# Routing by 32x32 block transposes, two score buffers for the first pairs, and one of five sums left to an accumulating DMA

## The chip, the cores and the metric

The kernel runs on one core of a Trainium2 chip. The metric is the device time of one execution in microseconds (us); lower is better. Engines: TensorE (PE, matmuls; its weight loads are shown apart as PEld), VectorE (DVE), ScalarE (ACT), GpSimd (POOL) and SyncE (SP), which issues most DMAs.

## The reference

Two stages. The first is attention in which a query sees only the keys of its own cluster; the second is a gated long convolution over the sequence. B, H, S, D = 4, 8, 768, 64; 16 centroids per head; model width 512.

```
q_assign = argmax(normalized q . normalized centroids)     # likewise k_assign
scores   = where(q_assign == k_assign, q k^T / 8, -1e9)
attn     = exp(scores - max) / sum
x        = (attn v), heads side by side                     # 4 x 768 x 512
x1, x2, x3 = split(x @ w_proj)
y        = x1 * irfft(rfft(x2) * rfft(filter)) * x3         # over the 768 steps
out      = y @ w_out                                        # float32
```

## The kernel before, in words

**Pairs and steps.** The 32 (batch, head) items are taken as 16 pairs of heads (p = 0 to 15, four pairs per batch). A pair has six steps of 128 keys (`attend`, sk = 0 to 5). A step computes the scores of 128 keys against 768 queries for both heads into three PSUM banks (L687, the matmuls through the helper `halves` at L324, which splits each into two of 64 columns), one exponential of 128x1536 on ACT into a buffer pb (L689; three such buffers), the products with v accumulated over the six steps in two other banks (PV, L699), and from the second step on a sum acc += pb on DVE (L709), five per pair, which gives the softmax denominators.

**Routing** (`routing`, L593 to L668). Per pair: q and k are loaded into raw (L384), transposed on PE (L606) and copied into qkT; POOL casts them into aug (L313). Similarities to the centroids are matmuls (L623) laid out as four groups of 32 partitions (query/key by half of the sequence). Then ACT or DVE copies them to sim (L626), PE transposes that in three blocks of 128 (L631), DVE takes the maximum and makes a one-hot with ties broken by a reversed index (L636 to L642), PE transposes the one-hot in six blocks (L650), and DVE or ACT scales it by mk into ohT (L655, L657): the query side becomes +-262144, the key side 0 or 1. Four DMAs (L664) put ohT's rows into aug beside q and k, so that the score matmul adds a large negative number where clusters differ; the scores wait for them.

**Finish** (`finish`, L715). Matmuls with ones sum acc over the keys (L728), and for pairs 0 to 14 the denominators go out and back through DRAM in five DMAs on SP (L733 to L740) with the reciprocal between (L736). The last pair does this with DVE's block transpose (L752, L762) instead. The normalized output becomes sums and differences uT (L769) and a bf16 copy xT.

**Second stage** (`hyena`, L775), once per batch after its four pairs: projections u, a real transform as matmuls (F) with DVE products tm and their sum, gates (G) into x13, an inverse transform in two parities pe and po (I, 16 matmuls per block of 128 columns, L853), which ACT copies (od) and DVE adds and subtracts (L860), the gate product (L863), and the output matmuls with w_out. `angles`, `inverse_tables` and `filter_tables` build the transform tables at the start.

**The order.** Nothing here is in the order in which it is written. Each piece is an `op` with engines that may take it, an estimated duration, dependences and a due time; `Plan.run` (L175) schedules all of them by a list, simulating engines, buffers and PSUM banks with those estimates, and issues the instructions in that order. Dues are worked back from each step's (`step`, L375). The constants at L26 to L30 set paces, the weight of waiting (WAIT) and a bonus for keeping the PE tile shape (SAME). Each engine then runs its own queue in order, with semaphores for the dependences. `BankPool.choices` (L92) says which of eight PSUM banks a value may use: scores only 0 to 2, PV 3 and 4, the rest 5 to 7 and whatever is left over before the first scores and after the last.

Of the kernel before, what the change touches and what calls it, by code (L numbers as in the profile page):

```python
# [13 lines left out]
F32 = mybir.dt.float32  # L14
# [15 lines left out]
SAME, WAIT, ANGLES = 1.08, 82.17, 0.99  # L30
# [44 lines left out]
class Banks:  # L75

    def __init__(self, scores, outs, rest):
        self.views = [scores[:, 512 * n:512 * n + 512] for n in range(3)]  # L80
        self.views += [outs[:, 512 * n:512 * n + 512] for n in range(2)] + rest
        self.whole = {"S": scores, "O": outs}
        self.free, self.owner = [0.0] * 8, [None] * 8
        self.scores_left = self.scores_begun = 0
        self.outs_left = 0


class BankPool:
# [3 lines left out]
    def choices(self):  # L92
        b, k = self.b, self.kind
        if k == "S":
            return [(0, 1, 2)]
# [7 lines left out]
        if not b.scores_left:  # L103
            ok += [0, 1, 2]
# [12 lines left out]
    def take(self, v, c):  # L117
        for n in c:
            self.b.owner[n] = v
        t = self.b.views[c[0]] if len(c) == 1 else self.b.whole["O" if c[0] == 3 else "S"]  # L120
# [12 lines left out]
class Op:  # L133
    __slots__ = ("alts", "fn", "deps", "succ", "need", "due", "vals", "takes", "mode", "lag", "size",
                 "end", "n", "shared", "ready", "kind", "after", "left", "table")


class Plan:
# [5 lines left out]
    def __init__(self):  # L144
        self.ops = []

    def op(self, engine, dur, fn, r=(), w=(), due=1e9, takes=(), mode=None, size=0, shared=False,
# [4 lines left out]
        o.left, o.table = left or mode, table  # L152
# [112 lines left out]
def kernel(  # L265
# [55 lines left out]
    def halves(out, lhsT, rhs, **k):  # L321

        for c in range(2):
# [7 lines left out]
    mk = const("mk", [64, 2])  # L331
# [5 lines left out]
    hm = const("hm", [128, 3, 4, DM], BF16)  # L337
    zeroed = Val(Pool("zeroed", [None]))
# [9 lines left out]
    ohTp = pool("ohT", 2, [64, S], BF16)  # L348
# [21 lines left out]
                  [psum.tile([128, 512], F32, name=f"bank{i}") for i in range(3)])  # L370
    psS, psO, psF, psD, psE = (BankPool(banks, x) for x in ("S", "O", "F", "D", "E"))
    banks.scores_left, banks.outs_left = NP * NT, NP
# [16 lines left out]
    def load_pair(p):  # L389
        b, h = p // 4, 2 * (p % 4)  # L390
        for j, src in enumerate((q, k)):
            x = raws[p, j] = Val(raw)
            for hp in range(2):
                load(lambda x=x, hp=hp: x.t[:, :, hp], src[b, h + hp].rearrange("(p t) d -> p t d", t=NT),
                     196608, step(6 * p - LOAD) + j if p else -1000.0, (x, hp),
                     after=step(6 * p - LOAD) - 8.0 if p > 1 else 0.0, behind=masks0)
        x = vraws[p] = Val(vraw)
# [4 lines left out]
    def constants():  # L402
        op("POOL", 0.5, lambda e: make_identity(nc, identp.t), w=[identp], kind="const")
# [3 lines left out]
        for g, (a, c) in enumerate(((BIG, -BIG), (1.0, 0.0))):  # L407
            def f(e, g=g, a=a, c=c):
                nc.gpsimd.memset(mk.t[32 * g:32 * g + 32, 0:1], a)
                nc.gpsimd.memset(mk.t[32 * g:32 * g + 32, 1:2], c)  # L410
# [4 lines left out]

    def zeros():
        def f(e):
# [9 lines left out]
    def centroid():  # L427
        small = {n: const(n, [128, w]) for n, w in
# [25 lines left out]
    def angles():  # L454


        N = 2 * 192
        na, ra = Val(k6), Val(k6)
# [19 lines left out]
        for m in range(3):  # L478
            n = lambda m=m: na.t[:, N * (m + 1):N * (m + 2)]
            r = lambda m=m: ra.t[:, N * m:N * (m + 1)]  # L480
            due = ANGLES + 1.5 * m
            op("DVE", 0.36, lambda e, m=m, n=n: V.tensor_scalar(n(), kc(), st.t[:, m:m + 1], None, op0=Alu.mult),
               r=[(na, "k"), st], w=[(na, m)], due=due)
            op("DVE", 0.36, lambda e, n=n, r=r: V.tensor_scalar(r(), n(), 1.0 / S, MAGIC, op0=Alu.mult, op1=Alu.add),
               r=[(na, m)], w=[(ra, m)], due=due)
            op("DVE", 0.36, lambda e, r=r: V.tensor_scalar(
                r(), r(), MAGIC, -float(S), op0=Alu.subtract, op1=Alu.mult), r=[(ra, m)], w=[(ra, m)], due=due)
            op("DVE", 0.56, lambda e, n=n, r=r: V.tensor_tensor(n(), n(), r(), op=Alu.add),
               r=[(ra, m)], w=[(na, m)], due=due, shared=True)
            done.append(op("DVE", 0.56, lambda e, n=n, r=r: V.scalar_tensor_tensor(  # L490
                r(), n(), -1.0, n(), op0=Alu.mult, op1=Alu.max), r=[(na, m)], w=[(ra, m)], due=due, shared=True))
        two = lambda x: x.rearrange("p (a b) -> p a b", a=2)
# [15 lines left out]
    def inverse_tables(due):  # L508
        for j in range(6):
            ps = Val(psF)  # L510

            def f(e, j=j, ps=ps):
# [11 lines left out]
               r=[ps], w=[inv], due=due + j + 1)  # L524

# [10 lines left out]
    def filter_tables(due):  # L536
        lo, hi, ud = Val(k6), Val(k6), Val(k6)
# [7 lines left out]
        op("DVE", 1.76, lambda e: nc.vector.tensor_tensor(fu(), lo.t, hi.t, op=Alu.add),  # L545
           r=[lo, hi], w=[(ud, 0)], due=due, shared=True)
        op("DVE", 1.76, lambda e: nc.vector.tensor_tensor(fd(), lo.t, hi.t, op=Alu.subtract),
# [10 lines left out]
        V = nc.vector  # L558
        for i in range(3):
            for cs in range(2):  # L560
                ps = Val(psF)
# [4 lines left out]
                op("DVE", 0.68, lambda e, i=i, cs=cs, ps=ps, w=w: V.tensor_scalar(  # L566
                    hm.t[:, i, 2 * cs], ps.t, w(), None, op0=Alu.mult), r=[ps, wt], w=[(hm, (i, 2 * cs))],
                   due=due + 2 * i + cs)
                if i == 0 and cs == 0:
                    op("DVE", 0.68, lambda e, ps=ps: V.tensor_scalar(  # L570
                        d1.t[:, 0], ps.t, wt.t[:, 1:2], None, op0=Alu.mult), r=[ps, wt], w=[d1], due=due)
# [4 lines left out]
                elif cs == 0:  # L576
                    op("DVE", 0.68, lambda e, i=i, ps=ps: V.tensor_scalar(
                        hm.t[:, i, 3], ps.t, 2.0 / S, None, op0=Alu.mult), r=[ps], w=[(hm, (i, 3))],
# [355 lines left out]
```

## Time and profile before

| what | us |
| --- | --- |
| median of 3 runs | 423.12 (422.86 to 423.76) |
| the profiled execution's own time | 422.92 |
| its span in the trace | 421.1 |
| PE busy / DVE busy / ACT busy / POOL busy | 393.9 / 354.4 / 256.5 / 120.9 |

The mean granted PE clock of the span is 0.984. A row of a group reads: line, engine, operation, output and inputs with shapes, count, then busy time in us and the mean of one in ns, then the idle time of the engine ahead of it and what ended that. A row in order of time reads: start in us, duration, engine, line, operation and count, and in brackets the idle time before it. The queue of SP shows as SPq.

### The profile page before, as it was taken

What the parts mean: (1) busy time and instruction counts of PE and PEld (TensorE: products, weight loads), DVE (VectorE), ACT (ScalarE), POOL (GpSimd) and SP (SyncE); (2) the same over time, 40 slices, a digit from 0 to 9 for tenths busy, and PEclk for the clock granted to TensorE, in tenths of its full rate; (3) what the DMA queues carried; (4) which work ended last, traced back from release to release, by engine and by line L of the source; (5) the groups of instructions that cost most, each with busy time, mean ns of one, the idle gap of its engine ahead of it and who ended that gap; (6) DMA issues with size and microseconds to landing.
All of it is one profiled execution on the core that took longest, in us unless ns stands there. A gap on an engine that the chain in (4) does not pass through costs nothing. (4 is left out here: it accounts for less than half of the span.)

```text
span 421.1 us, 8711 instructions
## 1 busy us (share of the span) xinstructions
PE 393.9 (94%) x3485; PEld 213.6 (51%) x3485; DVE 354.4 (84%) x414; ACT 256.5 (61%) x317; POOL 120.9 (29%) x114
## 2 busy tenths in 40 slices
PE   4489998999999999999999999999999999998794
PEld 2245444445445565655454545545655467555442
DVE  5959977898989898989879799999899788947673
ACT  2477655888577767555775766666676654344242
POOL 5722333155253140532405051407113002101000
PEclk9869999999999999999999999999999999999998
DMA  8199956544363314020365711110311002200123
GB/s 183 20 226 216 222 128 148 129 99 93 87 158 86 84 45 115 10 77 3 76 161 161 164 40 48 48 40 4 84 41 40 3 10 81 101 2 2 75 76 149
DMA packets 68943, 37.17 MB, mean 88 GB/s; under 512 B 56940, under 2 KB 62632, under 8 KB 68904
## 3 DMA queue, kind: packets, MB, share of 16 engines
q1 hardware_dynamic: 67640, 34.45, 31.9%
q0 software_dynamic: 1056, 2.10, 2.7%
q8 instruction: 27, 0.44, 0.4%
q10 hardware_dynamic: 208, 0.08, 0.1%
q14 instruction: 12, 0.10, 0.1%
HBM read 30.66 MB, written 6.48 MB: 88 GB/s over the span
## 5 line engine op out<-in xcount | busy, mean ns | idle before, releaser
L689 ACT ACTIVATE pb<-scores 128x1536 f32<-128x1536 f32 x96 | 139.4, 1452 | 52.2 <-PE scores L324 50.9
L699 PE MATMUL outs<-pb,vraw 128*64 128x512 f32 (+1 forms) x768 | 143.2, 492 | 0.2 <-ACT osb L719 0.2
L313 POOL CAST aug<-qkT 64x768 bf16<-64x768 f32 x64 | 85.1, 1329 | 160.6 <-PE scores L324 80.3
L709 DVE TENSOR_TENSOR acc<-acc,pb 128x1536 f32<-128x1536 f32 x64 | 118.1, 1845 | 9.5 <-ACT pb L689 9.1
L699 PEld LDWEIGHTS outs<-pb,vraw 128*64 128x64 f32 x768 | 54.4, 137 | 66.2 <-issue 59.7
L324 PE MATMUL scores<-aug,aug 128*64 128x512 bf16 (+3 forms) x768 | 81.8, 332 | 5.1 <-DMA aug<-ohT 2.8
L324 PEld LDWEIGHTS <-aug 80*64 80x64 bf16 (+1 forms) x768 | 42.1, 111 | 35.0 <-issue 15.5
L324 PEld LDWEIGHTS <-wpj 128*64 128x64 bf16 x512 | 32.3, 110 | 16.6 <-issue 5.6
L324 PE MATMUL bank<-xT,wpj 128*64 128x384 bf16 x384 | 38.5, 326 | 0.0
L709 DVE TENSOR_TENSOR acc<-pb,pb 128x1536 f32<-128x1536 f32 x16 | 31.8, 1987 | 4.7 <-ACT pb L689 4.7
L606 PE MATMUL bank<-ident,raw 128*128 128x128 f32 x183 | 30.5, 294 | 5.5 <-DMA raw<-in_q_dram 5.4
L324 PEld LDWEIGHTS <-k 128*64 128x64 bf16 (+1 forms) x448 | 21.7, 108 | 22.3 <-issue 11.4
L863 POOL TENSOR_TENSOR k<-yy,x 128x768 bf16<-128x768 f32 x7 | 16.1, 2302 | 58.6 <-DVE yy L860 54.1
L606 PEld LDWEIGHTS bank<-ident,raw 128*128 128x128 f32 x183 | 20.6, 147 | 20.1 <-issue 11.5
L311 ACT COPY qkT<-bank 128x384 f32<-128x384 f32 x47 | 21.8, 482 | 10.3 <-PE bank L606 10.2
L313 POOL CAST xT<-rb 128x768 bf16<-128x768 f32 x8 | 10.6, 1325 | 45.3 <-PE bank L324 20.1
L769 DVE TENSOR_TENSOR uT<-rb 128x384 bf16<-128x384 f32 x32 | 21.4, 680 | 0.1
L324 PE MATMUL bank<-wpj,uT 128*64 128x512 bf16 x160 | 20.6, 380 | 0.0
L804 DVE TENSOR_TENSOR tm<-bank,hm 128x1024 f32<-128x1024 f32 x16 | 19.4, 1219 | 0.8 <-PE bank L533 0.7
L719 ACT COPY osb<-outs 128x769 f32<-128x769 f32 x16 | 12.8, 801 | 8.9 <-PE outs L699 8.9
L764 DVE SCALAR_TENSOR_TENSOR rb<-osb,rb 128x768 f32<-128x768 f32 x16 | 17.8, 1114 | 0.0
L324 PEld LDWEIGHTS <-uT 128*64 128x64 bf16 x192 | 12.6, 109 | 8.6 <-issue 1.9
(161 smaller groups left out, 440.6 us busy)
## 6 DMA issues: line engine op xcount, KB each, us to landing
raw<-in_q_dram SPq DMA_DIRECT2D x32, 192.0 KB
raw<-in_k_dram SPq DMA_DIRECT2D x32, 192.0 KB
vraw<-in_v_dram SPq DMA_DIRECT2D x16, 384.0 KB
rb<-dr SPq DMA_DIRECT2D x30, 192.0 KB
out_dram<-os SPq DMA_DIRECT2D x21, 256.0 KB
k<-in_moe_filter_fft_dram SPq DMA_DIRECT2D x4, 384.0 KB
wpj<-in_moe_w_proj_dram POOLq DMA_DIRECT2D x1, 1536.0 KB, 14.3
aug<-ohT SPq DMA_DIRECT2D x62, 24.0 KB
```

The source lines that it names most:

```text
L311: nc.scalar.copy(o, i)
L313: eng[e].tensor_copy(o, i)
L324: nc.tensor.matmul(out[64 * c:64 * c + 64], lhsT[:, 64 * c:64 * c + 64], rhs, **k)
L606: nc.tensor.transpose(ps.t[:, ts(t, 128)], rv[:, 3 * ch + t], identp.t)
L689: op("ACT", 1.48, lambda e: nc.scalar.activation(pb.t[:, :, :S], sps.t.rearrange("p (a b) -> p a b", a=2), Act.Exp, scale=0.125), r=[sps], ...
L699: nc.tensor.matmul(o.t[64 * hp:64 * hp + 64, lo:hi], vv.t[:, hp, ts(sk, D)], pb.t[:, hp, lo:hi], start=(sk == 0), stop=(sk == NT - 1))
L709: nc.vector.tensor_tensor(acc.t, a, pb.t[:, :, :S], op=Alu.add)
L719: op("ACT", 0.82, lambda e: nc.scalar.copy(osb.t, o.t[:, :S + 1]), r=[o], w=[osb], due=step(i) + 5.0)
L764: op("DVE", 0.98, lambda e: V.scalar_tensor_tensor(rb.t, osb.t[:, :S], osb.t[:, S:S + 1], rb.t, op0=Alu.add, op1=Alu.mult), r=[osb, rb], w ...
L769: op("DVE", 0.55, lambda e, e_=e_, alu=alu: V.tensor_tensor(uT.t[:, e_], x3()[:, :, :64], x3()[:, :, 64:], op=alu), r=[rb], w=[(uT, e_)], ...
L804: op("DVE", 1.2, lambda e, i=i, cs=cs, ps=ps, tm=tms[cs]: V.tensor_tensor(tm.t, ps.t.unsqueeze(1).to_broadcast([128, 2, DM]), hm.t[:, i, c ...
L863: op(("DVE", "POOL"), (0.95, 1.8), lambda e, dt=dt, yt=yt, x13=x13: eng[e].tensor_tensor(y2v()[:, dt], yt().rearrange("p t c -> p (t c)"), ...
```

## The change

- **Routing.** The similarities go from PSUM to sim by DVE's transpose of 32x32 blocks; because they are laid out in groups of 32 partitions, this is all that the maximum needs. The one-hot goes back the same way. PE's two transposes and ACT's copy are gone. ohT becomes 128x384 (was 64x768), mk is scaled in place, and eight DMAs of half the length place the mask.
- **First scores.** In the first 24 steps scores may also use banks 5 to 7, and other values may use 0 to 2.
- **Sums.** In pairs 0 to 14 the fifth sum (sk = 5) is a DMA issued by POOL that adds pb into acc.
- **Inverse.** For batch 3, each parity is six matmuls straight into PSUM, with negated tables (`minus`, made on POOL), and DVE multiplies by x13 from PSUM; no od, yy or separate product.
- **Start.** 8 and 6 pairs of warm-up matmuls on the identity (`warm`); POOL may do parts of `angles` and of the filter's sum and difference, ACT parts of `filter_tables`.
- **Order.** Every op has a tag, and a table NUDGE adds a number to its due time; SAME is 2.358 (was 1.08), WAIT 145.939 (was 82.17).

```
+DIRECT = (3,)
+ADDED = (5,)
+TWICE = 24
+SAME, WAIT, ANGLES = 2.358, 145.939, 0.99
+NUDGE = {
+    "const": -13.63, "cent": -14.24, "l0.0": -135.15, "l0.1": -111.3, "v0": 25.44, "l1.0": -76.86,
...
+        o.due += NUDGE.get(o.tag, 0.0)
...
         if k == "S":
-            return [(0, 1, 2)]
+            return [(0, 1, 2)] + ([(5, 6, 7)] if b.scores_begun < b.twice else [])
...
-        if not b.scores_left:
+        if not b.scores_left or 0 < b.scores_begun < b.twice:
             ok += [0, 1, 2]
...
+    def warm(at, n, due):
+        for _ in range(n):
+            ps = Val(psE)
+            def f(e, ps=ps):
+                halves(ps.t, identb.t, identb.t.unsqueeze(1).to_broadcast([128, 4, 128]), start=True, stop=True)
+            op("PE", 0.43, f, r=[identb], w=[ps], due=due, after=at, mode="C64", kind="warm")
...
-        op(("ACT", "DVE"), (0.486, 0.55), lambda e: copy(e, sim.t, ps.t[:, :384]), r=[ps], w=[sim], due=due)
-                nc.tensor.transpose(sT.t[:, ts(t, 128)], sim.t[:, ts(t, 128)], identp.t)
+        op("DVE", 0.56, lambda e: nc.vector.transpose(sim.t, ps.t[:, :384]), r=[ps], w=[sim], due=due, kind="T1")
...
-                nc.tensor.transpose(tp[:64, t * 128:(t + 1) * 128], ov[:, t % 3, t // 3], identb.t)
+        op("DVE", 0.55, lambda e: V.transpose(ohT.t, oh.t.rearrange("p n c -> p (n c)")), r=[oh], w=[ohT], due=due,
+           kind="T2")
...
-        op(("DVE", "ACT"), (0.68, 0.815), f, r=[oT, mk], w=[ohT], due=due)
+        op(("DVE", "ACT"), (0.22, 0.48), f, r=[mk, ohT], w=[ohT], due=due)
...
-                    eng[e].dma_start(aug.t[hp][j][64 - 16 * hp:80 - 16 * hp], ohT.t[r0:r0 + 16])
+                for ch in range(2):
+                        r0 = 64 * ch + 32 * j + 16 * hp
+                        eng[e].dma_start(aug.t[hp][j][64 - 16 * hp:80 - 16 * hp, ts(ch, 384)], ohT.t[r0:r0 + 16])
...
-            op("DVE", 1.75, f, r=[pb] + ([last] if sk == 1 else [acc]), w=[acc], due=step(i) + 5.0,
-               shared=True, kind="acc")
+            if sk in ADDED and p < NP - 1:
+                op("POOL", 1.1, lambda e: nc.gpsimd.dma_start(acc.t, pb.t[:, :, :S], accum_op=Alu.add),
+                   r=[pb, acc], w=[acc], due=step(i) + 4.0, lag=7.0, kind="accD")
...
+            if b in DIRECT:
+                for e_ in range(2):
+                        for n in range(6):
+                            w = minus.t[:, n - 2] if e_ and n > 1 else inv.t[:, n]
+                            halves(ps.t[:, :384], yv()[:, n // 2, n % 2, ts(dt, 128)], w, start=(n == 0), stop=(n == 5))
...
+    warm(0.0, 8, FIRST - 300.0)
     routing(0)
+    warm(14.0, 6, T0 - 4.0)
```

More of the change, by code (lines that the diff above doesn't have):

```diff
@@ L79, in __init__ @@
     def __init__(self, scores, outs, rest):
[L80 to L82 removed]
+        self.views = [x[:, 512 * n:512 * n + 512] for x, m in ((scores, 3), (outs, 2), (rest, 3)) for n in range(m)]
+        self.whole = {0: scores, 3: outs, 5: rest}
         self.free, self.owner = [0.0] * 8, [None] * 8
[L84 removed]
+        self.scores_left = self.scores_begun = self.twice = 0
         self.outs_left = 0
@@ L134 @@
     __slots__ = ("alts", "fn", "deps", "succ", "need", "due", "vals", "takes", "mode", "lag", "size",
-                 "end", "n", "shared", "ready", "kind", "after", "left", "table")
+                 "end", "n", "shared", "ready", "kind", "after", "left", "table", "tag")
 class Plan:
@@ L369 @@
     banks = Banks(psum.tile([128, 1536], F32, name="scores"), psum.tile([128, 1024], F32, name="outs"),
-                  [psum.tile([128, 512], F32, name=f"bank{i}") for i in range(3)])
+                  psum.tile([128, 1536], F32, name="rest"))
     psS, psO, psF, psD, psE = (BankPool(banks, x) for x in ("S", "O", "F", "D", "E"))
-    banks.scores_left, banks.outs_left = NP * NT, NP
+    banks.scores_left, banks.outs_left, banks.twice = NP * NT, NP, TWICE
     def step(i):
@@ L720, in finish @@
         V = nc.vector
+        P.tag = f"den{p}"
         if p < NP - 1:
```

193 lines of the change are left out of this document (117 added, 76 removed), and 68 rows, old and new, of the table NUDGE.

## The prediction

> **What bounds the kernel now.** The first view is the page: busy time by engine, then the slices of the span.
>
> ```profile
> PE 393.9 (94%) x3485; PEld 213.6 (51%) x3485; DVE 354.4 (84%) x414; ACT 256.5 (61%) x317; POOL 120.9 (29%) x114
> ...
> PE   4489998999999999999999999999999999998794
> ...
> PEclk9869999999999999999999999999999999999998
> ```
>
> TensorE (PE) is busy for 393.9 of 421.1 us, and its row of tenths is full except at both ends. VectorE (DVE) is the runner-up with 84%. The averages hide stages, so the second view is the table of busy time by stretch; its columns are stretch, length, then PE, weight loads, DVE, ACT and POOL with counts, the granted PE clock and the DMA share.
>
> ```profile
> 80.00:100.00 20.00, 20.00 (x157) 9.22 (x153) 18.30 (x18) 15.86 (x17) 9.89 (x6) 1.00 0.38 85
> ...
> 360.00:380.00 20.00, 18.85 (x204) 11.16 (x200) 13.28 (x22) 8.43 (x16) 0.02 (x1) 1.00 0.14 52
> 380.00:400.00 20.00, 15.31 (x162) 10.00 (x157) 14.72 (x15) 6.77 (x15) 1.81 (x1) 1.00 0.11 40
> ```
>
> In the middle PE has no gap at all, at full clock, while DVE is at 18.3 of 20. In 360 to 400 PE is idle for 1.15 + 4.69 = 5.84 us: there the last batch waits for chains on DVE. So an instruction taken from PE in the middle is worth its whole time, one taken from DVE is worth nothing until something on PE or ACT waits for it, and the ends are about latency.
>
> **What leaves PE.** The routing loses its two transposes on PE: three of the similarities (L631) and six of the one-hots (L650) in each of 16 pairs. From the groups by line and shape:
>
> ```profile
> L709 DVE TENSOR_TENSOR acc<-acc,pb 128x1536 f32<-128x1536 f32 x64 | 118.1, 1845 | 9.5 <-ACT pb L689 9.1
> ...
> L631 PE MATMUL bank<-ident,sim 128*128 128x128 f32 x45 | 8.2, 291 | 0.0
> L650 PE MATMUL bank<-identb,oh 128*64 128x128 bf16 x90 | 7.9, 226 | 1.3 <-DVE oh L642 1.3
> ...
> L655 ACT ACTIVATE ohT<-bank,mk 64x768 bf16<-64x768 bf16 x7 | 6.9, 981 | 0.3 <-PE bank L650 0.3
> ...
> L311 ACT COPY sim<-bank 128x384 f32<-128x384 f32 x13 | 6.2, 478 | 7.9 <-PE bank L623 7.9
> ...
> L657 DVE TENSOR_SCALAR ohT<-bank,mk 64x768 bf16<-64x768 bf16 x8 | 5.3, 667 | 2.9 <-PE bank L650 2.8
> ...
> L752 DVE STREAM_TRANSPOSE acc<-scores 128x768 f32<-128x768 f32 x1 | 1.0, 983 | 1.4 <-PE scores L324 1.4
> ```
>
> Busy times of matmuls overlap, so I take distances between starts, in order of time:
>
> ```profile
> 150.15 1.59 PE L699 MATMUL outs<-pb,vraw 128*64 128x512 f32 x8
> 151.67 0.55 PE L631 MATMUL bank<-ident,sim 128*128 128x128 f32 x3
> 152.15 0.84 PE L324 MATMUL scores<-aug,aug 80*64 80x512 bf16 x8
> ...
> 166.63 1.46 PE L699 MATMUL outs<-pb,vraw 128*64 128x512 f32 x8
> 167.92 0.82 PE L324 MATMUL bank<-xT,wpj 128*64 128x384 bf16 x8
> ...
> 169.22 0.39 PE L650 MATMUL bank<-identb,oh 128*64 128x128 bf16 x4
> ...
> 169.56 1.46 PE L533 MATMUL bank<-k,fw 128*64 128x512 bf16 x11
> ```
>
> L631 occupies 152.15 - 151.67 = 0.48 us, L650 169.56 - 169.22 = 0.34. The eight PV matmuls ahead of L631 take 1.52, ahead of another 64-column matmul 167.92 - 166.63 = 1.29, so the change of tile shape costs about 0.2 more. That is 1.02 us for each of the 15 pairs behind the first: **-15.3 us**. Its bounds are 0 (PE then waits for what takes its place) and -17 (the busy times of both rows, with three missing and six missing records).
>
> **What goes to DVE and ACT.** Per pair DVE gains two block transposes of 384 columns; the nearest row is L752, 768 columns in 0.983, so about 0.5 each (bounds 0.25 and 1.0, half and all of that row), and a scaling of 384 columns near 0.2 to 0.5. It loses L657 in half of the pairs, 0.33 on average. Net +0.9 us, 14 in all. ACT loses the copy of sim (0.478) and L655 in half of the pairs (0.49). The fifth sum goes from DVE to the accumulating DMA in 15 pairs: 15 x 1.845 = 27.7 us. So DVE ends near 354 + 14 - 28 = 340. Since PE covers DVE in the middle, this is cost **0**; if that cover goes, the DVE order is late next (a rival below). The mask goes out in eight DMAs in place of four on SP's queue, some 2.4 us more of issue per pair, ahead of the denominators' four DMAs and the loads; with six steps per pair SP has room.
>
> **Alternating scores.** Two consecutive exponentials are never closer than this:
>
> ```profile
> 59.64 1.45 ACT L689 ACTIVATE pb<-scores 128x1536 f32<-128x1536 f32 x1 [0.69 <-PE scores L324]
> 69.11 1.45 ACT L689 ACTIVATE pb<-scores 128x1536 f32<-128x1536 f32 x1 [1.88 <-PE scores L324]
> 71.49 1.45 ACT L689 ACTIVATE pb<-scores 128x1536 f32<-128x1536 f32 x1 [0.56 <-PE scores L324]
> ...
> 147.10 1.45 ACT L689 ACTIVATE pb<-scores 128x1536 f32<-128x1536 f32 x1
> ...
> 153.09 1.45 ACT L689 ACTIVATE pb<-scores 128x1536 f32<-128x1536 f32 x1 [0.95 <-PE scores L324]
> ...
> 343.51 1.45 ACT L689 ACTIVATE pb<-scores 128x1536 f32<-128x1536 f32 x1 [1.08 <-PE scores L324]
> ```
>
> 71.49 - 69.11 = 2.38: exp, scores, exp on one buffer is a loop. From 69.11 to 147.10 are 28 steps, 2.79 each; from 153.09 to 343.51 are 54, 3.53 each, with the filter stage between them. With 0.17 us per step less PE work the loop would soon bind in the early pairs; the second buffer of scores in the first 24 steps lifts it. I count it as what lets those 15.3 us be had, and give it nothing of its own. Its price is three banks that the routing shares.
>
> **The accumulating DMA.** No row shows one. It is issued on POOL, waits there for the exponential and the fourth sum, and casts of q, k and xT queue behind it. It moves 768 KB. The nearest rows:
>
> ```profile
> wpj<-in_moe_w_proj_dram POOLq DMA_DIRECT2D x1, 1536.0 KB, 14.3
> ...
> 414.87 2.03 DMA out_dram<-os
> ...
> 415.00:420.00 5.00, 0.70 (x6) 0.14 (x3) 0.69 (x1) 1.51 (x3) 0.00 (x0) 0.77 0.83 315
> ```
>
> Lower end: a store of 256 KB lands in 2.03; the other 512 KB at 315 GB/s add 1.7: 3.7 us. Upper end: POOL's own load wpj, twice the bytes and cast, 14.3. I take 7.2, half of wpj, because it is the same queue and also reads twice what it writes. What it can hold up is the buffer pb: three exist, so three steps after the fifth exponential began its buffer is wanted again. Time allowed behind the end of the exponential: 3 x 2.79 - 1.45 = 6.9 us in the first 7 pairs, 3 x 3.53 - 1.45 = 9.1 in the other 8. At 7.2 the exponential is held 0.3 x 7: **+2 us**; at 3.7 it is 0; at 14.3 it is 7.4 x 7 + 5.2 x 8 = 93.
> By the Trainium skill, page "Collectives: The Full Stack", section "The bandwidth ceiling: the fold count and why AG ≠ RS ≠ AR", the adding DMA is held back by its two reads, not by the add; with the bandwidth in "DMA: Bandwidth & Descriptors", section "Anatomy of one DMA", an estimate is 2.0 + 2 x 786 KB / 436 GB/s = 5.6 us, and the +2 would be 0; no run here shows that yet.
>
> **Start.** The first routing in order of time, and two stretches with their clock:
>
> ```profile
> 15.00:20.00 5.00, 1.00 (x9) 0.67 (x9) 4.89 (x9) 2.04 (x3) 4.03 (x11) 0.83 0.05 11
> 20.00:25.00 5.00, 3.12 (x20) 1.98 (x21) 3.23 (x7) 3.73 (x4) 0.00 (x0) 0.50 0.85 204
> ...
> 11.35 0.48 ACT L311 COPY sim<-scores 128x384 f32<-128x384 f32 x1 [2.17 <-PE scores L623]
> ...
> 13.43 0.54 DVE L636 TENSOR_REDUCE mx<-scores 128x24 f32<-128x384 f32 x1
> ...
> 18.07 1.51 SPq L664 DMA_DIRECT2D aug<-ohT  x2
> ...
> 20.34 1.49 PE L324 MATMUL scores<-aug,aug 80*64 80x512 bf16 x8 [2.85 <-DMA aug<-ohT]
> ```
>
> From 11.35 to 13.43 becomes one transpose of 0.5: -1.5. L655's 0.98 becomes a transpose and a scaling: -0.3. Two more mask issues per queue, 1.51 / 2 each: +1.5. The clock: after the gap in 15 to 20 PE runs at 0.50, and scores take 1.49 where 152.15 shows 0.84. Warm-up matmuls while PE waits, at 0 and at 14, would take back about half of the 3.12 busy us: -1.5, and as much again in the first transposes, -1.2. Sum **-3**, bounds 0 and -6.
> By the Trainium skill, page "TensorE: Matmul & The Clock Gate", Part 1, the clock comes back only after a window of about 3.4 us of activity and is lost after an idle one; the trace's 0.83 and then 0.50 behind the 1.00 us busy in 15 to 20 agrees with the loss. Six warm-up matmuls of 512 columns fill 2.6 us at half clock by that page, so they might not bring it back: the start would then be -1.5 and the sum 1.5 us longer.
>
> **Tail and order.** For the last batch the inverse goes direct. Now, per block:
>
> ```profile
> 404.82 1.27 PE L324 MATMUL scores<-inv,k 128*64 128x384 bf16 x16
> ...
> 405.09 1.02 DVE L860 TENSOR_TENSOR acc<-bank,od 128x384 f32<-128x384 f32 x2 [0.60 <-ACT od L311]
> 406.02 0.84 PE L324 MATMUL bank<-xT,wpj 128*64 128x384 bf16 x8
> 406.14 0.96 DVE L863 TENSOR_TENSOR k<-acc,x 128x768 bf16<-128x768 f32 x1
> ```
>
> 16 matmuls take 406.02 - 404.82 = 1.20; 24 full ones at 0.65 / 4 a pair (167.92's kind) take 1.95: +0.75 x 4 = +3 on PE. DVE loses 1.02 + 0.96 and gains 2 x 0.55, ACT loses the copy: -3.5 on the chain between. I set these off against each other. The table of nudges reorders everything; it can at best close the 5.84 us idle and at worst open gaps of like size. I take half of the best: **-3**, bounds -6 and +10. The four negated tables cost POOL some 4 us early, off the path.
>
> **The sum.** 421.1 - 15.3 + 2 - 3 - 3 = 401.8 for the span. The profiled execution took 422.92, 1.8 more than its span, and stands 0.2 under the median 423.12. So 403.6, rounded to **404 us**.
>
> **The rivals.**
> 1. *The DMA holds pb* (the other side). If it lands T after the exponential, the loss is 7 (T - 6.9) + 8 (T - 9.1), each only where positive. Without the +2 the sum is 401.6; the 21.3 us up to 422.9 are used up at T = 9.5. At T = 11 it is 28.7 + 15.2: 445 us. For it: ACT is in order, so copies for PE queue behind the held exponential, and wpj's 14.3. Against: 7.2 is nearer to both lower rows, and in the later pairs PE has other matmuls ready. Chance 0.20, from 424 up.
> 2. *POOL's issue waits for DVE.* If issuing stands behind one DVE instruction, 1.85 by L709, T is 9.05: 2.15 x 7 = 15, 417 us. Against: the trace has only two POOL issues and no such wait. Chance 0.08. The Trainium skill, page "SBUF — State Buffer", section "Who interferes with whom", gives the rule: descriptor generation by GpSimd is locked out by VectorE's two-port modes; no run here shows it.
> 3. *The routing is late instead.* All of it is now on DVE, at 18.3 of 20 in the early pairs; if masks come late, scores wait as in the 9.5 us between 59.64 and 69.11 of the exponentials, and 11 of the 15.3 go (the early 7 pairs and half of the others): about 415 us. Against: DVE loses 1.845 per pair at that place. Chance 0.10.
> 4. *The order closes more.* All 5.84 us of tail, all 6 of the start (3 more each) and some 18 changes of tile shape at 0.2: 394 us. Chance 0.12.
>
> My forecast, 398 to 412, has 0.48. The last 0.02 is a loss of just the gain. Faster by over 0.2% (about what a measurement here can tell from no change) is 0.48 + 0.08 + 0.10 + 0.12 = 0.78, same 0.02, slower 0.20. The range is 391 to 427: it leaves out the rest of rival 4 and rival 1 beyond T near 9.8.
>
> **What would show it.** Right: PE busy down to about 378, full tenths in the middle, no idle ACT ahead of exponentials released by the DMA, its landing below 8 us. Rival 1 shows as ACT or PE waits released by a DMA into acc, once per pair; rival 2 as POOL's issue long beside DVE; rival 3 as PE idle on masks. I am wrong if PE stays full and the time doesn't fall by 10, for then PE's time was not in those transposes.

## The result, and the profile after

The changed kernel takes **486.74 us** (median of 4 runs, 486.15 to 487.59) against 423.44 (422.86 to 424.06) for the kernel before on the same chip: a ratio of 1.150, with an interval of 1.147 to 1.152. It is 63 us slower where 19 less were forecast. Its span is 484.4 us. One execution of four of e9 and one of e15 below ran in a slower state, and their times are given without it.

The page of the changed kernel: busy time with its share of the span, the 40 slices, and the granted clock in the same slices.

```profile
PE 403.8 (83%) x3401; PEld 216.0 (45%) x3401; DVE 328.1 (68%) x409; ACT 247.3 (51%) x308; POOL 125.9 (26%) x142
...
PE   6475899989788678898889778899896878978796
...
PEclk9757899989999999999999999999999999999999
```

PE's row was full from the eighth slice to the 36th; now it moves between 6 and 9 from the fifth slice on. PE's idle time, span less busy, was 421.1 - 393.9 = 27.2 us and is 484.4 - 403.8 = 80.6. Its busy time, forecast to fall to about 378, rose to 403.8, at a mean granted clock of 0.967 (0.984 before). DVE and ACT are less busy than before, so no engine has become the bound: PE waits a little in almost every stretch. The same by stretch (stretch, length, then busy time and count of PE, weight loads, DVE, ACT and POOL, then granted clock, DMA share, GB/s):

```profile
80.00:100.00 20.00, 19.10 (x156) 9.39 (x154) 15.23 (x16) 15.66 (x17) 5.61 (x7) 1.00 0.67 136
160.00:180.00 20.00, 13.53 (x119) 7.31 (x121) 11.63 (x16) 8.57 (x12) 1.03 (x1) 1.00 0.47 105
360.00:380.00 20.00, 14.52 (x130) 8.08 (x126) 10.88 (x11) 10.04 (x12) 4.96 (x3) 1.00 0.37 86
```

The kernel before had from 160 to 180:

```profile
160.00:180.00 20.00, 20.00 (x194) 12.21 (x194) 17.96 (x15) 13.81 (x18) 6.36 (x4) 1.00 0.28 67
```

The loss is small from 80 to 100, before the first batch has its four pairs, and large where the second stage's projections run. All groups of matmuls that write the banks 5 to 7, now called `rest`, together have 52.8 us of PE's idle time just ahead of them (the sum of their rows); before, as `bank`, they had 7.2. Two of these groups alone have 25.6; the last column is the idle time.

```profile
L399 PE MATMUL rest<-xT,wpj 128*64 128x384 bf16 x408 | 41.7, 327 | 13.4 <-DVE tm L921 6.4 <-ACT k L386 2.4 <-DVE x L951 2.0
...
L399 PE MATMUL rest<-wpj,uT 128*64 128x512 bf16 x160 | 21.1, 381 | 12.2 <-ACT k L386 4.1 <-DVE sim L740 3.0 <-DVE k L388 1.8
```

The same two groups in the kernel before had no idle time at all:

```profile
L324 PE MATMUL bank<-xT,wpj 128*64 128x384 bf16 x384 | 38.5, 326 | 0.0
...
L324 PE MATMUL bank<-wpj,uT 128*64 128x512 bf16 x160 | 20.6, 380 | 0.0
```

One early loss is of another kind. From 40 to 60 PE is busy 12.13 us where it was 19.70, and the longest wait there (what PE waits for, then us in total, times, longest) is for a load of q, ahead of the transposes of a later pair:

```profile
PE scores L718 <- DMA raw<-in_q_dram: 6.3, 1, 6.3
```

A stretch of the changed kernel in order of time shows what the two groups wait for (start, duration, engine, line, operation; in brackets the idle time and who ended it):

```profile
163.33 1.05 PE L399 MATMUL rest<-wpj,uT 128*64 128x512 bf16 x8 [0.68 <-DVE qkT L388]
164.42 0.58 DVE L740 STREAM_TRANSPOSE sim<-rest 128x384 f32<-128x384 f32 x1 [1.15 <-PE rest L399]
...
165.05 1.05 PE L399 MATMUL rest<-wpj,uT 128*64 128x512 bf16 x8 [0.67 <-DVE sim L740]
...
166.15 0.59 ACT L386 CAST k<-rest 128x512 bf16<-128x512 f32 x1 [4.67 <-PE rest L399]
...
166.78 1.05 PE L399 MATMUL rest<-wpj,uT 128*64 128x512 bf16 x8 [0.67 <-ACT k L386]
```

This is strict alternation: eight matmuls into one bank (1.05 us), then a read of a bank by ACT or DVE (0.6), then the next eight. At 165.05 a projection of the second stage waits for `sim<-rest`, a step of the routing of quite another pair, which reads another bank than the one that the projection writes. The copy at 166.15 reads the bank that was filled at 163.33, and yet it begins behind the matmuls of 165.05, which fill a third. Nothing in the computation ties these. What ties them is one edit of the diff that the prediction passed over. The banks 5, 6 and 7 were three PSUM tiles of 512 columns; so that a score of 1536 columns can use them, they became one tile, and the banks became slices of it:

```
-[psum.tile([128, 512], F32, name=f"bank{i}") for i in range(3)]
+psum.tile([128, 1536], F32, name="rest")
+self.views = [x[:, 512 * n:512 * n + 512] for x, m in ((scores, 3), (outs, 2), (rest, 3)) for n in range(m)]
```

**The theory**: a matmul into one bank of this tile waits for the last reader of any bank of it, and the reader waits for the last writer, so three banks work as one. **The rivals**: the accumulating DMA holds buffers; the table of nudges and the new weights make a bad order; or the block-transposed routing loads DVE.

### The profile page after: what moved, and what is told of

Same layout as the page of the kernel before. It is cut to its first block, busy times and chain, and to the rows that moved or that the text cites. A ratio compares the mean times of both kernels' runs of the same rounds, so it can differ in the third digit from the quotient of the medians.

```text
span 484.4 us, 8642 instructions
## 1 busy us (share of the span) xinstructions
PE 403.8 (83%) x3401; PEld 216.0 (45%) x3401; DVE 328.1 (68%) x409; ACT 247.3 (51%) x308; POOL 125.9 (26%) x142
## 4 chain that ended last, share of the span: by engine, by line
PE 59%; DVE 14%; DMA 12%; ACT 9%; issue 3%; SPq 2%; DVEq 0%; ACTq 0%
PE rest L399 20%; PE outs L806 18%; PE scores L399 11%; DVE tm L921 4%; PE rest L718 3%; DMA raw<-in_q_dram 3%; DMA rb<-dr 3%; ACT pb L795 2%; DMA k<-in_moe_filter_fft_dram 2%; PE rest L842 2%; DVE x L951 2%; DMA dn<-dd 2%; ACT k L386 2%; DMA raw<-in_k_dram 2%; DVE acc L817 1%
## 5 line engine op out<-in xcount | busy, mean ns | idle before, releaser
L795 ACT ACTIVATE pb<-scores 128x1536 f32<-128x1536 f32 x84 | 122.0, 1453 | 55.3 <-PE scores L399 54.9
L388 POOL CAST aug<-qkT 64x768 bf16<-64x768 f32 x64 | 66.0, 1031 | 141.6 <-PE scores L399 116.8
L817 DVE TENSOR_TENSOR acc<-acc,pb 128x1536 f32<-128x1536 f32 x49 | 87.5, 1786 | 13.4 <-ACT pb L795 12.8
L399 PE MATMUL scores<-aug,aug 80*64 80x512 bf16 (+3 forms) x672 | 71.5, 330 | 6.4 <-ACT pb L795 3.3
L399 PE MATMUL rest<-xT,wpj 128*64 128x384 bf16 x408 | 41.7, 327 | 13.4 <-DVE tm L921 6.4
L921 DVE TENSOR_TENSOR tm<-rest,hm 128x1024 f32<-128x1024 f32 x21 | 25.6, 1222 | 27.3 <-PE rest L399 17.0
L386 ACT COPY qkT<-rest 128x384 f32<-128x384 f32 x38 | 16.9, 482 | 29.2 <-PE rest L718 16.3
L399 PE MATMUL rest<-wpj,uT 128*64 128x512 bf16 x160 | 21.1, 381 | 12.2 <-ACT k L386 4.1
L718 PE MATMUL rest<-ident,raw 128*128 128x128 f32 x138 | 21.8, 285 | 9.2 <-DVE sim L740 2.2
L819 POOL DMA_DIRECT2D acc<-pb x15 | 18.1, 1205 | 40.2 <-ACT pb L795 26.4
```

What stands on the lines that cost most here:

```text
L386: nc.scalar.copy(o, i)
L388: eng[e].tensor_copy(o, i)
L399: nc.tensor.matmul(out[64 * c:64 * c + 64], lhsT[:, 64 * c:64 * c + 64], rhs, **k)
L718: nc.tensor.transpose(ps.t[:, ts(t, 128)], rv[:, 3 * ch + t], identp.t)
L795: op("ACT", 1.48, lambda e: nc.scalar.activation(pb.t[:, :, :S], sps.t.rearrange("p (a b) -> p a b", a=2), Act.Exp, scale=0.125), r=[sps], ...
L817: nc.vector.tensor_tensor(acc.t, a, pb.t[:, :, :S], op=Alu.add)
```

## The experiments

### The three banks as one tile: e1, e3, e4, e9

**e1**: the kernel before, with only the edit above (three banks as slices of one tile). The order of instructions on every engine is that of the kernel before.

> The kernel before with one edit: the three other PSUM banks are slices of one tile of 1536 columns, as after the change, in place of three tiles. Every engine's order of instructions stays the same. Theory A (a matmul into one bank of this tile waits until the last reader of any of its banks is done): 450 to 485 us, with waits of PE on copies by ACT and DVE from this tile. Theory B (the accumulating DMA holds the buffers pb): no difference, 423 us. Theory C (the new order is bad on the chip): no difference, 423 us.

Measured: 484.61 us (482.26 to 486.82), ratio 1.142 (1.136 to 1.147). The one edit alone makes 61 us. Its profile, by stretch and by group:

```profile
80.00:100.00 20.00, 18.58 (x150) 9.87 (x152) 15.38 (x17) 14.80 (x17) 4.45 (x3) 1.00 0.40 94
160.00:180.00 20.00, 16.23 (x136) 8.33 (x133) 12.59 (x16) 9.18 (x11) 3.69 (x4) 1.00 0.10 26
```

```profile
L325 PE MATMUL rest<-xT,wpj 128*64 128x384 bf16 x384 | 38.8, 327 | 10.5 <-DVE tm L805 2.9 <-DVE x L834 1.6 <-ACT x L831 1.5
...
L325 PE MATMUL rest<-wpj,uT 128*64 128x512 bf16 x160 | 22.1, 393 | 6.4 <-DVE k L314 1.7 <-ACT k L312 1.4 <-DVE qkT L314 1.2
```

The groups that stood at 0.0 wait as in the changed kernel, and for the same mixture of readers: any DVE or ACT instruction that reads any of the three banks. In order of time:

```profile
164.72 1.92 PE L325 MATMUL rest<-wpj,uT 128*64 128x512 bf16 x16 [0.74 <-ACT k L312]
167.49 1.05 PE L325 MATMUL rest<-wpj,uT 128*64 128x512 bf16 x8 [0.85 <-DVE k L314]
169.21 1.05 PE L325 MATMUL rest<-wpj,uT 128*64 128x512 bf16 x8 [0.67 <-ACT k L312]
```

**e3 and e4**: the changed kernel without the second score buffer (`TWICE = 0`), once with the one tile and once with three. The two have the same order of instructions on every engine and the same banks, so they differ in nothing else.

```
-TWICE = 24
+TWICE = 0
-psum.tile([128, 1536], F32, name="rest")                                       (e4 alone)
+[psum.tile([128, 512], F32, name=f"bank{i}") for i in range(3)]                (e4 alone)
```

> The changed kernel with scores in their own three banks throughout (no second score buffer), the other three banks still slices of one tile. Theory A: 460 to 490 us. Theory B: 480 us or more. Theory C: near 487 us if the order is at fault, 410 if the second score buffer is.

> As the kernel before it, but with three tiles for the three banks, and exactly the same order on every engine. Theory A: 400 to 415 us, 50 us or more below its twin. Theory B: the same as its twin, 480 us or more. Theory C: the same as its twin.

Measured: 490.25 us, ratio 1.155 (1.150 to 1.160), with one tile; 440.65 (437.53 to 442.20), 1.037 (1.031 to 1.043), with three. The tile makes 50 us here too. The same instructions on the same banks do without these waits when the banks are three tiles, so the waits come from how the program's semaphores are placed, by tile, and not from a limit of the banks. Without the one tile the changed kernel is still 17 us slower than before.

**e9**: can the second score buffer be had without the one tile? The changed kernel in its own order, three tiles, and each of the twelve exponentials that read banks 5 to 7 split into three of 512 columns.

```
-Act.Exp of rest[:, :1536] in one instruction
+Act.Exp of bank5, bank6 and bank7, 512 columns each
```

> The changed kernel with its own order, instruction by instruction, but the three shared banks are three tiles; the 12 exponentials whose scores lie there become three of 512 columns each. If the one tile was the whole loss and the order is good: 395 to 412 us, the forecast without it. If the order is no better than that of the runs with three tiles and other orders: 430 to 442 us.

Measured: 439.96 us (435.47 to 441.65), ratio 1.035 (1.027 to 1.043). The tile costs 47 us here, and the second score buffer, freed of it but with its exponentials split, gives nothing over e4's 440.65. **The first theory stands**: the tile makes 47 to 61 us in three comparisons; two of them, e1 against the kernel before and e3 against e4, differ in nothing else. With three tiles 16 to 17 us are left (439.96 and 440.65 against 424).

### What is left: the DMA and the routing by themselves: e2, e10, e5, e6, e7, e8

**e2** and **e10**: no accumulating DMA, the fifth sum on DVE again (`ADDED = ()`), with the one tile and with three (as e9).

```
-ADDED = (5,)
+ADDED = ()
```

> The changed kernel with the fifth sum back on DVE in all pairs, the rest as it is (the planner orders anew). Theory A: still 460 to 490 us. Theory B: 400 to 410 us, the gain that was forecast without the DMA's price. Theory C: within 10 us of 487, since nudges and waits stay.

> As the kernel before it, with the fifth sum on DVE in all pairs (planned anew). If the DMA is what helps: 10 us or more above its twin. If the DMA holds pb: 10 us or more below.

Measured: 510.56 us, ratio 1.204 (1.199 to 1.210), with one tile, and 438.71, 1.036 (1.031 to 1.041), with three. With one tile the DMA saves 24 us against the sum on DVE; with three it changes nothing (439.96 against 438.71, whose intervals overlap). So the DMA isn't the cause of the 63 us. Both runs without it are planned anew, so the order differs too. Why it saves so much under the one tile is only argued: there every reader on DVE that comes late holds up PE, and the sum of 1.8 us stands ahead of readers.

**e5, e6, e7**: parts of the change on the kernel before, on three tiles: the block-transposed routing alone, the accumulating DMA alone, and both.

```
+V.transpose(sim.t, ps.t[:, :384]); V.transpose(ohT.t, oh.t); eight mask DMAs     (e5, e7)
+nc.gpsimd.dma_start(acc.t, pb.t[:, :, :S], accum_op=Alu.add)  for sk == 5, p < 15  (e6, e7)
```

> The kernel before with only the routing changed (block transposes on DVE, eight mask DMAs); three PSUM tiles, the old planner constants. My step on PE (1.02 us per pair leave it and nothing takes their place): 405 to 411 us. The rival that the routing comes late because DVE is full: 420 us or more.

> The kernel before with only the fifth sum of pairs 0 to 14 as an accumulating DMA. My step (landing near 7.2 us, little or no hold-up, DVE's 27.7 us hidden by PE): 418 to 427 us. The rival that the DMA holds pb: 435 us or more, with waits released by a DMA into acc.

> The kernel before with both the new routing and the accumulating DMA. If the two steps add as forecast: 403 to 411 us. If DVE was what the routing alone was short of, this is well below the routing alone; if the DMA holds pb, above it.

Measured: routing 436.00 us, ratio 1.029 (1.024 to 1.034); DMA 441.88, 1.045 (1.039 to 1.051); both 437.52, 1.034 (1.031 to 1.037). Each part costs by itself, and they don't add up: 13, 19, and 14 together. Neither gives any of the gain that the prediction's terms would have it give. For e6 the rival of a DMA that holds things up had named both 435 us or more and waits released by it; such waits are there, but small (what waits, then us in total, times, longest):

```profile
PE bank L732 <- DMA acc<-pb: 2.6, 4, 1.7
...
ACT pb L689 <- DMA acc<-pb: 1.7, 2, 1.1
```

**e8**: e4 without the table of nudges and with the old weights.

```
-SAME, WAIT = 2.358, 145.939
-NUDGE = {...}
+SAME, WAIT = 1.08, 82.17
+NUDGE = {}
```

> The changed kernel with three PSUM tiles, scores in their own banks, an empty table of nudges and the old SAME and WAIT; routing, DMA, direct inverse and warm-up stay. If the 440.65 of the run with three tiles came from nudges that fit another plan: 398 to 412 us. If it came from the direct inverse, the warm-up or the DMA: 430 us or more.

Measured: 435.81 us, ratio 1.030 (1.024 to 1.036), against 440.65 with the table. The table is not what costs: without it 13 us are left. That these are 5 fewer is not clear of the noise, as the intervals overlap.

### What does a new order cost by itself? e11, e12, e17

Each edit makes the planner order everything anew. Three kernels do the work of the kernel before in another order; a few pieces also change between ACT, DVE and POOL, as the planner may choose among them.

```
+SAME, WAIT = 2.358, 145.939                                       (e11)
+o.due += (len(self.ops) * 7919 % 101) / 101.0 - 0.5               (e12)
-ROUTE, LOAD, TABLES, FILTER = 3.96, 24.14, 0.98, 1.79
+ROUTE, LOAD, TABLES, FILTER = 9.96, 24.14, 0.98, 1.79             (e17)
```

> The kernel before with only the planner's SAME and WAIT of the change: the same work in another order. If the constants of the kernel before fit its own plan and any other order costs: 430 to 440 us, as the runs of single parts. If those runs lost their time to the parts themselves: 420 to 427 us.

> The kernel before with a fixed pseudo-random shift of up to half a microsecond on every due time: the same work, another order. If any other order costs: 430 to 440 us. If not: 420 to 427 us.

> The kernel before with its routing due 6 us sooner, as in run e16, and nothing else changed: the control for that run. If the 6.7 us that e16 gained over e5 belong to the block-transposed routing (its masks were late), this run gains nothing, 421 to 432 us. If the sooner routing helps any kernel of this kind, it is at 418 or under.

Measured: 425.76 us, ratio 1.0045 (1.0026 to 1.0064); 428.62, 1.011 (1.007 to 1.014); 430.07, 1.014 (1.006 to 1.021). So a new order of the same work costs 2 to 6 us, before any part of it has been made cheaper or dearer. That is less than the 430 to 440 that one theory of e11 and e12 expected; e12 lies between its two theories.

### Leaving work out: e13, e14

**e13**: the kernel before without the fifth sum in 15 pairs, and no DMA in its place. **e14**: the kernel before without the routing's two transposes, neither on PE nor on DVE, with the eight mask DMAs of the change.

```
-op("DVE", 1.75, ...acc...)  for sk == 5, p < 15                    (e13)
-nc.tensor.transpose(sT...), nc.tensor.transpose(tp...)             (e14)
```

> The kernel before with the fifth sum of exponentials left out in 15 of 16 pairs (its denominators lack one of six terms); no accumulating DMA stands in its place, and the planner orders the rest anew. It gives what those 27.7 us of VectorE are worth if they cost nothing elsewhere. If the 19 us that the DMA alone added (run e6) belong to the DMA, to its landing and to what waits for it, this run is at the kernel before or under it, 410 to 426 us. If they belong to the order that the planner makes once VectorE has less to do, this run is slow as well, over 433. By the prediction's step 'VectorE is covered by TensorE' it is within some 2 per cent of 423, never faster than 415.

> The kernel before with the routing's two transposes left out altogether: TensorE loses them as in the change, but VectorE gets no block transpose in their place (the copy of sim stays, the mask scaling reads the one-hot as it is), so the routing's choice of buckets is not that of the reference. Masks go out in eight DMAs as in run e5. By the prediction's step for TensorE this is 15 us under the kernel before, 405 to 411 us. If VectorE's added transposes made the 13 us that run e5 lost, it is under 426 too. If what costs is that TensorE's work was no bound there, or the order and the eight masks, it is at 430 or over.

Measured: 431.98 us, ratio 1.020 (1.017 to 1.022), and 429.78, 1.015 (1.012 to 1.018). e13 lies between what two of its theories expected and within the 2 per cent that DVE under PE's cover allows, and e14 just under the 430 of its second. **Less work, and slower**, on DVE (27.7 us of sums gone) as on PE. What PE saved in e14 it lost again as idle time. Its busy time on the page:

```profile
PE 385.6 (90%) x3341; PEld 195.5 (46%) x3341; DVE 353.3 (83%) x412; ACT 254.5 (60%) x317; POOL 119.3 (28%) x120
```

That is 393.9 - 385.6 = 8.3 us less than before, in a span that is 426.4 - 421.1 = 5.3 longer: 13.6 us more of idle PE. Two stretches hold 10.2 of them:

```profile
40.00:60.00 20.00, 13.63 (x97) 5.84 (x94) 18.25 (x25) 6.94 (x9) 6.69 (x4) 0.92 0.91 194
280.00:300.00 20.00, 15.88 (x138) 8.20 (x136) 18.98 (x20) 10.50 (x12) 6.78 (x5) 0.89 0.08 26
```

The kernel before had in the same two:

```profile
40.00:60.00 20.00, 19.70 (x171) 9.67 (x166) 19.86 (x21) 12.40 (x14) 4.19 (x3) 1.00 0.90 191
280.00:300.00 20.00, 20.00 (x192) 11.38 (x190) 18.55 (x18) 12.87 (x14) 9.60 (x6) 1.00 0.12 30
```

PE loses 6.1 us in the first and 4.1 in the second, with DVE at 18.3 and 19.0 of 20. The waits of PE in e14 (what it waits for, then us in total, times, longest) that fall in them are for DVE, whose queue is at that time full of the filter's tables (`tm`, `hm`) and of the second stage's products (`x`):

```profile
PE bank L716 <- DVE x L821: 3.9, 1, 3.9
...
PE bank L716 <- DVE hm L577: 2.2, 1, 2.2
PE bank L324 <- DVE tm L570: 2.2, 1, 2.2
```

### Sooner, and with longer delays: e16, e18, e15

**e16** and **e18**: e5 and e7 with the routing due 6 us sooner (the edit of e17). **e15**: e6 with the planner told 10 us for the accumulating DMA (7 before) and 4 for each hop of the denominators (2 before).

```
+ROUTE, LOAD, TABLES, FILTER = 9.96, 24.14, 0.98, 1.79              (e16, e18)
+lag=10.0 for accD; lag=4.0 for dd, dn, dr                          (e15)
```

> Run e5 (the block-transposed routing alone, 436.0 us) with the routing of each later pair due 6 us sooner (9.96 in place of 3.96 ahead of the pair's first step). If the loss is that the masks come late because the routing queues on VectorE, it falls to 428 or under. If the order as such or VectorE's total is at fault, it stays within 5 us of 436 or rises.

> Run e7 (block-transposed routing and accumulating DMA on three separate tiles, 437.5 us) with the routing due 6 us sooner. If late masks make part of the loss there too, 427 to 433 us; if the DMA's waits make it, within 4 us of 437.5. No theory expects it under the kernel before, for e14 showed TensorE's transposes to be worth nothing and e13 VectorE's sum as well.

> Run e6 (the accumulating DMA alone, 441.9 us) with the planner told longer delays: 10 in place of 7 us for the accumulating DMA, 4 in place of 2 for each of the three hops of the denominators through memory. So it puts more work ahead of what waits for them. If the loss is VectorE and TensorE standing in order behind instructions that were placed too early for their DMAs, it falls by 8 us or more, to 434 or under. If it is the DMA's traffic or any new order, it stays within 5 us of 442.

Measured: e16 429.29 us, ratio 1.014 (1.012 to 1.017), 6.7 under e5; e18 437.46, 1.030 (1.022 to 1.038), the same as e7; e15 450.33 (448.80 to 452.36), 1.064 (1.060 to 1.069), 8.4 above e6. A sooner due takes 6.7 us off the block-transposed routing, just short of what the theory of late masks expected (428 or under), while it costs the kernel before 6.4 (e17). Whether something in e5 comes too late, and whether it is the masks, is asked below; orders alone differ by 2 to 6 us. With that due the block-transposed routing (429.29) is level with the routing on PE (430.07). e18 came out as the DMA's waits would have it, and in e7 PE stands 5.5 us once, in e18 4.4, until an accumulating DMA has landed. For the DMA both expectations of e15 missed: told longer delays, the planner made it worse. No kernel here beats the one before.

## Why the prediction was wrong, by its steps

**Alternating scores: this step failed first.** The prediction gave it nothing and put "its price is three banks that the routing shares". The sharing it thought of was of time on the banks. The price was that the three banks became one tile and lost their independence: +61 (e1), +50 (e3 against e4), +47 (the change against e9). The gain it was to make possible isn't there either: freed of the tile, e9 is level with e4. No rival held this. They asked which engine or DMA comes late; here engines waited for each other in turn without need.

**PE's 15.3 us: failed as well.** The prediction argued that PE is busy 94%, full in the middle, "so an instruction taken from PE in the middle is worth its whole time". e14 takes exactly these and gains nothing; e5, which moves them to DVE, loses 13. The lower bound given, 0 "(PE then waits for what takes its place)", is where it lies or beyond, but the waits were not for what takes its place: e14 has nothing in its place. PE and DVE were both near full in 40 to 60 and in 280 to 300, and the kernel before had them interlocked there without a gap. My reading, from these two stretches alone, is that with a piece taken from one and the order made anew the gap opens at the other; no run shows it by itself. How much of e14's 6.6 us is the order and how much the lack of a gain can't be told apart, since a new order alone costs 2 to 6.
By the Trainium skill, page "Trainium Kernel Development and Optimization", section "Performance Expectations", matmul busy time is a bad metric of how close a kernel is to its limit, because matmuls are pipelined. e14 agrees that busy time is no measure of the time: it fell by 8.3 us and the time rose. That pipelining is the reason no run here shows; what e14 lost is idle time.

**DVE at cost 0 under PE's cover: neither borne out nor refuted.** The block transposes took what was estimated, in the changed kernel:

```profile
L754 DVE STREAM_TRANSPOSE ohT<-oh 128x384 bf16<-128x384 bf16 x16 | 9.1, 571 | 0.3
L740 DVE STREAM_TRANSPOSE sim<-rest 128x384 f32<-128x384 f32 x13 | 7.5, 579 | 11.7 <-ACT hm L669 5.1 <-PE rest L399 3.6 <-PE rest L737 2.2
```

0.57 and 0.58 us, against "about 0.5 each". At the old due, e5 with them (436.00) is 6 us over e14, which has no transposes at all (429.78). At the sooner due they cost nothing that can be seen: e16 429.29, e17 430.07. One gap of e5 lies between 43 and 56 us. PE waits there, and its clock falls to 0.51:

```profile
46.92 0.84 PE L324 MATMUL bank<-k,fw 128*64 128x512 bf16 x6 [1.60 <-DVE tm L570]
...
48.24 1.49 PE L533 MATMUL bank<-k,fw 128*64 128x512 bf16 x6 [0.48 <-DVE hm L573]
...
51.31 1.51 PE L718 MATMUL bank<-acc,ones 128*32 128x384 f32 x8 [1.57 <-DVE hm L577]
```

```profile
45.00:50.00 5.00, 2.65 (x16) 0.84 (x12) 5.00 (x8) 0.00 (x0) 2.06 (x2) 0.80 1.21 223
50.00:55.00 5.00, 3.69 (x22) 0.76 (x22) 5.00 (x11) 1.20 (x2) 0.00 (x0) 0.51 0.89 213
```

These waits are for the filter's tables on DVE, not for a mask, and e14, without a transpose on DVE, has the same three (2.2, 0.5 and 2.2 us). Rival 3, "the routing is late instead", would show as PE idle on masks. In e5 PE waits for one once, at the first pair's scores (what it waits for, then us in total, times, longest):

```profile
PE scores L324 <- DMA aug<-ohT: 5.8, 1, 5.8
```

The kernel before waited 2.8 there, and e16 still waits 5.9. So rival 3 isn't seen behind the first pair, and what the 6.7 us are that a sooner due takes off e5 **stays open**.

**The accumulating DMA: the landing was right, its price was not.** On the page and in the transfers of the changed kernel:

```profile
L819 POOL DMA_DIRECT2D acc<-pb x15 | 18.1, 1205 | 40.2 <-ACT pb L795 26.4
```

```profile
acc<-pb POOLq DMA_DIRECT2D x15, 768.0 KB, 7.4
```

7.4 us from issue to landing (the median; 6.4 to 8.2) where 7.2 was taken. The issue mostly comes 0.3 us behind the exponential, so the landing is near 7.7 behind it and rival 1's point of 9.5 isn't reached. No wait of the changed kernel is released by this DMA. Its issue takes 1.2 us in the mean, so rival 2 isn't seen. On three tiles it does release waits of PE, of the matmuls that sum acc: 5.4 us in e4, 5.5 in e7. That path, through the denominators, the prediction left out; it priced only the buffer pb. In e6 the landing is near 8.1 behind the exponential, for which the prediction's formula gives 7 x 1.2 = 8; the exponentials wait for it 1.7 in all.
By the Trainium skill, page "Collectives: The Full Stack", section "The bandwidth ceiling: the fold count and why AG ≠ RS ≠ AR", the two reads set the pace, and the prediction's estimate with them was 5.6; the measured 7.4 is longer, and decides.
Yet the DMA alone (e6, 441.88) is 10 us over the same kernel with the sum simply left out (e13, 431.98), which is also in another order. One place of e6 shows how it can act through the denominators:

```profile
80.56 0.58 SPq L737 DMA_DIRECT2D dd<-den  x1
...
85.61 0.23 DVE L740 RECIPROCAL dn<-dn 128x12 f32<-128x12 f32 x1 [6.17 <-DMA dn<-dd]
...
86.63 4.04 DVE L709 TENSOR_TENSOR acc<-acc,pb 128x1536 f32<-128x1536 f32 x2
...
88.48 1.45 ACT L689 ACTIVATE pb<-scores 128x1536 f32<-128x1536 f32 x1 [3.46 <-DVE acc L709]
...
89.98 1.49 PE L324 MATMUL scores<-aug,aug 80*64 80x512 bf16 x8 [2.77 <-ACT pb L689]
```

The denominators now start after the DMA. They were ready at 73.08, but their first hop left SP's queue only at 80.56, behind five loads of q, k and v. The reciprocal waits 6.17 us at the head of DVE's queue for the second hop; two sums stand behind it and keep the buffers pb, the exponential waits 3.46 for one, and PE 2.77 for the exponential, after which its scores take 1.49 in place of 0.84. The buffer is held, as in rival 1, but by DVE. This is one place, read from a trace. e15 was to heal it with longer delays in the plan and made it worse, so **the cause of these 10 us stays open**; the waits that this DMA releases itself add up to 4.3.

**Start, -3.** Part of it came. The changed kernel's first transposes, first scores and first exponential, in order of time:

```profile
5.13 0.84 PE L718 MATMUL rest<-ident,raw 128*128 128x128 f32 x6
...
17.95 0.52 PE L399 MATMUL scores<-aug,aug 80*64 80x512 bf16 x4 [2.08 <-POOL aug L514]
...
18.45 1.28 ACT L594 ACT_TABLE_LOAD   x1 [4.90 <-DVE k L584]
...
19.70 1.54 PE L399 MATMUL rest<-aug,aug 80*64 80x512 bf16 x8
...
21.00 1.61 ACT L591 ACTIVATE fw<-k,quarter 128x384 bf16<-128x384 f32 x3
...
22.63 1.28 ACT L795 ACT_TABLE_LOAD   x1
...
23.92 1.45 ACT L795 ACTIVATE pb<-scores 128x1536 f32<-128x1536 f32 x1
```

The kernel before:

```profile
5.40 1.51 PE L606 MATMUL bank<-ident,raw 128*128 128x128 f32 x6 [5.40 <-DMA raw<-in_q_dram]
...
21.87 1.45 ACT L689 ACTIVATE pb<-scores 128x1536 f32<-128x1536 f32 x1 [1.24 <-PE scores L324]
```

The warm-up in front of the first transposes worked: six of them take 0.84 us and not 1.51. The first scores start at 17.95 and not at 20.34. The second warm-up, at 14.39, did not hold the clock: the second step's scores take 1.54, and the granted clock from 20 to 40 is 0.52 where it was 0.79. The prediction had allowed for that with 1.5 us. And the first exponential comes 2.05 us later (23.92 against 21.87), since ACT was given the sines of the transform's tables, with two loads of its function table, ahead of it. So the term is +2 in place of -3: that the new order moves work on ACT too was not looked at.

**Tail and order, -3.** The table and the weights of the order give no gain: 440.65 with them, 435.81 without (e4, e8), which is +5 at most, inside the upper bound of 10. The direct inverse wasn't tried alone.

**The sum**: of the 63 us, 47 to 61 are the tile. The rest can be told apart only for the parts alone: of the routing's 13, a sooner due takes off 7, and the 6 that are left are as many as e17 loses by its order alone; the DMA's 19 are 9 for an order with less on DVE (e13) and 10 that stay open. Why both together cost 14 and not more isn't known. The sentence "I am wrong if PE stays full and the time doesn't fall by 10" named the wrong sign: PE did not stay full, and the time rose.

## What to carry to other kernels

Read a diff of PSUM for what becomes one tile: in these runs the waits follow the tile, not the bank or the columns, and a merge made for one user of 1536 columns chained every user of 512. A full row of busy time on one engine does not say that its work has a price: when a second engine is nearly full beside it, leave the work out in a run before counting on it. And where an order is computed, measure first what a harmless new order costs; here that was 2 to 6 us, as much as most of the terms that were being weighed.

## What the runs showed of the hardware

An accumulating DMA of 768 KB from one buffer of the core to another lands 7.4 us after its issue in the changed kernel (the median of 15; 6.4 to 8.2) and costs POOL 1.2 us of issue each time. In the runs on three tiles the median is 6.7 to 7.8, and single ones reach 12.0 (e7). After gaps in PE's work the granted clock in a stretch of 5 us is down to about half (0.51 in e5 at 50 to 55, behind a stretch in which PE was busy 2.65 of 5 us), so a wait of PE can cost more than its length: the score matmuls that follow the 2.77 us wait in e6 take 1.49 where 0.84 is usual, and the clock from 90 to 95 there is 0.69. Eight pairs of matmuls on the identity, from 1.61 us on, were enough for six transposes at 5.13 to take 0.84 in place of 1.51.
